# Several changes at once to a tuned attention-plus-MLP kernel: early identity matmuls, 128-wide K/Q transposes, 64-row score tiles, a product in spare PSUM, and new orders of work

## The chip, the cores and the metric

One core of one Trainium2 chip. The metric is device time in microseconds (us), as the median of several executions. PE is the matmul engine, PEld its weight loads, DVE the vector engine, ACT the activation engine, POOL the general engine that also issues the casting DMAs, SP the engine that issues the other DMAs. Ratios are the mean time of one kernel's fast runs over the mean of the other's fast runs of the same rounds, so they are not quite the ratios of the medians quoted.

## The reference

Block-sparse attention (4 batches, 8 heads, 768 positions of 64 values, blocks of 32), followed by a two-layer MLP with exact gelu on its output.

```
mask = |block_i - block_j| <= 1, or either block is the first or the last,
       or block_j is one of 3 sampled blocks of block_i
attn = softmax(where(mask, q @ k.T / 8, -1e9)) @ v         # per batch and head
x    = attn, heads side by side: 3072 x 512
out  = gelu(x @ w_in) @ w_out                              # w_in 512 x 2048, w_out 2048 x 512
```

## The kernel before

Work is cut into eight halves of a batch (384 rows). While PE does the MLP of half n, it also does the attention of half n+1, and POOL gathers K and V blocks for the halves after that. Each half has an order string, whose tokens are played one after the other and fix each engine's order: `H` is a step of the first MLP product (`hp`), `O` of the second (`op`), `S` scores, `W` weighted values, `D` and `E` scores and values of the two end blocks of queries, `t`/`u` transposes of the next batch's K/Q, `K`/`C` gathers of K and V on POOL, `L` the K/Q loads of a batch (on POOL), `F`/`f` scores of batch 0, `B`/`R` the cast of the next batch's V and its rotated copies.

```python
SPARSE = """
H H Z H H B H O1 H H O1 H O2 S0 O1 t1 K01 O3 W0 S1 O1 t0 X0 O2 W1 u0 S2 ... """

def load_qk(b, which, n):                       # 4 heads of a batch, cast f32 -> bf16 by the DMA
    t = st_pool.tile([P, NPAIR, NT * D], BF16, tag="st", name="st")
    pool.dma_start(out=t, in_=src[b, 4 * n:4 * n + 4].rearrange("h (p j) d -> p h (j d)", j=NT))
    return t                                    # rows of 6 * 64 floats: 1,536 bytes

# transpose_qk: two heads of 64 columns go to the upper and the lower half of PSUM
for j in range(NT):
    for h in range(2):
        pe.transpose(ps[64 * h:64 * h + 64, j, :], pair[:, h, j * D:j * D + D], ident)

# dense_scores: qgl holds the end queries of two heads block-diagonally (POOL copies them there)
for t in range(NT):
    pe.matmul(sd[:, t // 3, t % 3 * P:t % 3 * P + P], lhsT=st["k", hp][:, t * P:t * P + P],
              rhs=qgl[hp], start=True, stop=True)

# hidden_steps: products 0/1 and 2/3 take the two score tiles of PSUM, 4/5 waits for a gelu to free one
def step(m):
    mms(m, range(KIN - 1, KIN) if m < 4 else range(KIN))
    gelu(m)
```

The softmax here doesn't subtract the row's maximum and nothing guards it: scores larger than these inputs give would overflow.

Of the kernel before, what the change touches and what calls it, by code (L numbers as in the profile page):

```python
# [10 lines left out]
F32 = mybir.dt.float32  # L11
BF16 = mybir.dt.bfloat16
# [3 lines left out]
AF = mybir.ActivationFunctionType  # L16
ALU = mybir.AluOpType
AX = mybir.AxisListType

P = 128  # L20
B, H, S, D = 4, 8, 768, 64
BLOCK = 32
NB = S // BLOCK
NT = S // P
NR = 3
# [3 lines left out]
NPAIR = H // 2  # L29
# [9 lines left out]


VCH = (4, 4, 3)


class InOrder:
# [12 lines left out]


OPENING = """
A0 F00 k1 F01 F02 q1 F03 F04 F05 k3 P0 F10 F11 F12 k2 q2 F13 J0 F14 F15 F20 V00 V01 V02 F21 J1 F22 q3 F23 F24 F25 X0 F30 V10 V11 V12 P1 F31 F32 J2 F33 X1 V20 V21 V22 J3 F34 M1 F35 X2 V30 V31 L1 V32 H X3"""  # L60
FIRST = """
H H m0 I0 m1 m2 I1 H H m3 m4 H I2 I3 H H I4 H O2 I5 O1 f00 O2 f01 m5 f02 O2 I6 I7 F03 F04 V00 O1 F05 f10 V01 O1 f11 V02 f12 f13 O2 f14 f15 O1 V10 O1 X0 F20 F21 u0 V11 V12 B F22 F23 V20 O1 t0 f24 f25 O1 X1 V21 O1 f30 F31 u1 V22 F32 O2 t1 f33 F34 O1 V30 f35 K00 X2 O1 I8 O1 V31 V32 Q0 O1 R Q1 H K01 X3 O2"""
SECOND = """
H t2 H u3 t3 C00 H C01 C02 H G H H H M2 H K02 O2 K03 S0 u2 K11 K10 C10 C11 O4 D0 O2 L2 W0 S1 O3 D1 X0 C12 O1 E0 W1 S2 O2 E1 O1 X1 K12 D2 O1 W2 S3 O2 X2 E2 D3 O1 W3 E3 O2 K13 Y X3 O3 H"""
SPARSE = """
H H Z H H B H O1 H H O1 H O2 S0 O1 t1 K01 O3 W0 S1 O1 t0 X0 O2 W1 u0 S2 X1 O1 K00 R O2 C00 O1 C01 C02 u1 W2 S3 O2 X2 O3 W3 H O2 X3 O2"""
DENSE = """
M3 H H t2 u2 H H H t3 u3 H H H O2 K03 K02 O1 L3 K10 S0 O1 C10 O2 D0 O1 G O1 W0 S1 O1 K12 O2 C11 D1 O1 X0 W1 C12 S2 O2 E0 K13 O1 D2 O1 E1 W2 S3 O1 K11 O1 X1 E2 D3 O1 W3 E3 O2 Y X2 O3 X3 H"""
SPARSE2 = """
H H Z H H B H O1 H H O1 H O2 S0 O1 t1 K01 O3 W0 S1 O1 t0 X0 O2 W1 u0 S2 X1 O1 K00 R O2 C00 O1 C01 C02 u1 W2 S3 O2 X2 O3 W3 H O2 X3 O2"""  # L70
DENSE2 = """
H H t2 u2 H H H t3 u3 H H H O2 K03 K02 O1 K10 S0 O1 C10 O2 D0 O1 G O1 W0 S1 O1 K12 O2 C11 D1 O1 X0 W1 C12 S2 O2 E0 K13 O1 D2 O1 E1 W2 S3 O1 K11 O1 X1 E2 D3 O1 W3 E3 O2 Y X2 O3 X3 H"""
LAST_SPARSE = """
H H H Z H O1 H H H H O2 S0 O5 S1 W0 O5 W1 S2 O1 X0 X1 O3 W2 S3 O4 X2 O1 W3 H X3 O2"""
LAST = """
H H H O2 H H O2 H H H O28"""
ORDERS = (OPENING, FIRST, SECOND, SPARSE, DENSE, SPARSE2, DENSE2, LAST_SPARSE, LAST)


# [1 line left out]
def kernel(  # L81
# [34 lines left out]
    def cast(eng, dst, src):  # L116
        (eng.copy if eng is act else eng.tensor_copy)(dst, src)


    def load_qk(b, which, n):  # L120

        t = st_pool.tile([P, NPAIR, NT * D], BF16, tag="st", name="st")
        src = {"q": q, "k": k}[which]
        pool.dma_start(
            out=t, in_=src[b, 4 * n:4 * n + 4].rearrange("h (p j) d -> p h (j d)", j=NT))
        return t

    def load_v(b, eng):
# [41 lines left out]
    def small(name, shape, dtype=F32, home=msk):  # L170
        return home.tile([P] + shape, dtype, name=name)
# [11 lines left out]
    iota(blocks, [[1, NB]], 0, 0)  # L183


    kg_all = small("kg_all", [2, NPAIR, NQH, P], BF16, const)
    pt_all = small("pt_all", [2, 2, 2, 512], BF16, const)
    onehot = pt_all[:, 0].rearrange("p a h c -> p (a h c)")[:, 0:NB * BLOCK]
# [18 lines left out]
    dve.memset(seen[:, NB - 1:NB], 1.0)  # L207

    kgl = [[small(f"kgl{i}{hp}", [P], BF16, const) for hp in range(NPAIR)] for i in range(2)]
    qgl = [small(f"qgl{hp}", [P], BF16, const) for hp in range(NPAIR)]  # L210
    vgl = [small(f"vgl{i}", [NPAIR, 2 * VW], BF16, const) for i in range(2)]
    n_all = (NAT1 + NT) * H * GW
    v_flat = small("v_flat", [2 * -(-n_all // DW) * DW], BF16, const)
# [6 lines left out]
    dve.tensor_copy(raw_b, raw[:, :, :, 0].rearrange("p n s -> p (n s)"))  # L220
    ps_raw = mm_pool.tile([P, NB * NR], F32, tag="mm", name="ps_raw")
    pe.matmul(ps_raw, lhsT=ones, rhs=raw_b, start=True, stop=True)
    dve.tensor_copy(sbf.rearrange("p n s -> p (n s)"), ps_raw)
    dve.tensor_scalar(hit, sbf, key_b[:, 0:1], None, op0=ALU.is_equal)
    for s in range(NR):
        dve.tensor_add(seen, seen, hit[:, :, s])
    dve.tensor_scalar(barred.rearrange("p (n c) -> p n c", c=BLOCK),
                      seen.unsqueeze(2).to_broadcast([P, NB, BLOCK]),
                      0.5, -30000.0, op0=ALU.is_lt, op1=ALU.mult)

    lane_i = small("lane_i", [4], I32)
    lane = small("lane", [4])
# [25 lines left out]
                       in_=v[0, 4 * i:4 * i + 4].rearrange("h (p j) d -> p h (j d)", j=NT))  # L258
    for c in range(2):
        load_w_in(c)  # L260
    dve.memset(v_own[0][:, :, :, D:2 * GW], 1.0)

    def first_own(hp):
        r = slice(2 * hp, 2 * hp + 2)
        dve.tensor_copy(v_own[0][:, :, r, 0:D],
                        first_v[:, r].rearrange("p h (j d) -> p j h d", d=D))
# [150 lines left out]
    def transpose_qk(b, hp, which, pair, eng, st):  # L417

        dst = qkt_pool.tile([P, S], BF16, tag=f"t{which}", name=f"t{which}")
        home = (og_pool, "og") if b == 0 and which == "q" else (mm_pool, "mm")  # L420
        ps = home[0].tile([P, NT, P], BF16, tag=home[1], name="ps")
        for j in range(NT):
            for h in range(2):
                pe.transpose(ps[64 * h:64 * h + 64, j, :], pair[:, h, j * D:j * D + D], ident)
        if b == 0 and which == "k":
            to, frm, n = dst.rearrange("p (j n) -> p j n", j=NT), ps, NT
        else:
            to, frm, n = dst.rearrange("p (n j) -> p n j", j=NT), ps.rearrange("p j n -> p n j"), P
        for e, lo, hi in eng if isinstance(eng, tuple) else ((eng, 0, 1),):
            c = slice(int(lo * n), int(hi * n))  # L430
            cast(e, to[:, c], frm[:, c])
        st[which, hp] = dst

    def globals_qk(b, hp, which, eng, st):
        gl = kgl[b % 2][hp] if which == "k" else qgl[hp]
        for i in range(2):
            rs = slice(64 * i, 64 * i + 64)
            cast(eng, gl[rs, rs].rearrange("p (n c) -> p n c", n=2),
                 st[which, hp][rs, :].rearrange("p (n c) -> p n c", c=BLOCK)[:, 0::NB - 1, :])

    def gather_k(b, hb, hp, st):
        kg = st["kg", hb, hp] = kg_all[:, hb, hp]
# [37 lines left out]
    def dense_scores(hp, st):  # L480

        pd = p_pool.tile([P, NT, P], BF16, tag="pd", name="pd")
        sd = sc_pool.tile([P, 2, 512], F32, tag="sc", name="sd")
        for t in range(NT):
            pe.matmul(sd[:, t // 3, t % 3 * P:t % 3 * P + P], lhsT=st["k", hp][:, t * P:t * P + P],
                      rhs=qgl[hp], start=True, stop=True)
        act.activation(pd.rearrange("p (a t) c -> p a (t c)", a=2), sd[:, :, 0:3 * P],
                       AF.Exp, scale=scale)
        st["pd", hp] = pd

    def normalise(dst, og, n):
# [115 lines left out]
    def hidden_steps(b, hb, st):  # L607
        xT = st["xT", hb]

        held = {}  # L610

        def mms(m, kis):
            if 0 in kis:
                held[m] = sc_pool.tile([P, 2, 512], F32, tag="sc", name="hp")
            for i in range(2):
                for ki in kis:
                    pe.matmul(held[m][:, i, 0:HALF], lhsT=w_in_sb[:, ki, (m + i) * P:(m + i + 1) * P],
                              rhs=xT[:, ki, :], start=(ki == 0), stop=(ki == KIN - 1))

        def gelu(m):  # L620
            if m == 0:
                st["g", hb] = g_pool.tile([P, KOUT, HALF], BF16, tag="g", name="g")
            act.activation(st["g", hb][:, m:m + 2, :], held.pop(m)[:, :, 0:HALF], AF.Gelu)

        def begin():
            for m in (0, 2):
                mms(m, range(KIN - 1))

        def step(m):
            mms(m, range(KIN - 1, KIN) if m < 4 else range(KIN))  # L630
            gelu(m)

        return [begin] + [lambda m=m: step(m) for m in range(0, KOUT, 2)]

# [32 lines left out]
    def first_pair(hp, which="kq"):  # L667
        for w in which:
            pair = st["st", w, hp // 2][:, 2 * (hp % 2):2 * (hp % 2) + 2, :]
            if hp == 0:  # L670
                cast(act if w == "k" else dve, pair, first_st[w])
        for w in which:
            pair = st["st", w, hp // 2][:, 2 * (hp % 2):2 * (hp % 2) + 2, :]
            transpose_qk(0, hp, w, pair, (((dve, 0, 1 / 3), (act, 1 / 3, 1)) if w == "k" else ((dve, 0, .5), (act, .5, 1)))
                         if hp == 0 else dve, st)
# [4 lines left out]
                sts[b]["st", w, n] = load_qk(b, w, n)  # L680

    def transpose_next(b, hp, w):
        transpose_qk(b, hp, w, sts[b]["st", w, hp // 2][:, 2 * (hp % 2):2 * (hp % 2) + 2, :],
                     dve, sts[b])
        globals_qk(b, hp, w, pool, sts[b])

    def own_step(b):
        for i in range(2):
# [11 lines left out]
        sts[b]["st", "v"] = load_v(b, pool if b == 1 else sp)  # L700

    def clear_keys():
        for t in kgl[0] + kgl[1] + qgl:
            dve.memset(t, 0.0)

    def clear_values():
# [102 lines left out]
```

## Time and profile before

288.22 us is the median of 3 runs (288.1 to 288.62). The page's first part gives busy time, share of the span and instruction count of each engine:

```profile
PE 265.4 (93%) x3453; PEld 163.5 (57%) x3495; DVE 142.0 (50%) x375; ACT 162.5 (57%) x215; POOL 95.1 (33%) x134
```

PE is the engine to look at, but busy PE time is not PE at its peak, so the main reading was of steps: the time from the start of a group of matmuls to the start of the next group. The timeline of PE shows two matmul groups around a set of K transposes (start, length, engine, operation, count):

```profile
119.66 0.38 PE L54 MATMUL op<-w_out_sb,g 128*128 128x512 bf16 x1
119.97 0.53 PE L54 MATMUL ps<-ident,st 128*64 128x128 bf16 x12
120.43 0.82 PE L54 MATMUL op<-w_out_sb,g 128*128 128x512 bf16 x3
```

Twelve half-width transposes hold PE from 119.97 to 120.43, 0.46 us, of which the last one alone accounts for 0.15 (a tail of 0.12; the others step 0.028 each). The `op` matmul ahead of them takes 0.31 us to the next start, where others take 0.216. So here a change between full-width and half-width tiles cost about 0.09 us before the group and 0.12 after it.

The waits view, for PE (who waited for whom: total us, times, longest), in its first rows:

```profile
PE ps_raw L54 <- DVE raw_b L54: 3.7, 1, 3.7
PE hp L54 <- ACT g L54: 2.5, 5, 0.6
```

All its PE rows together are 15.0 us. The second row is the third product waiting for a gelu to free a score tile: 0.57 us early in each of four halves (2, 4, 6 and 7), and 0.2 us some 7 us into half 1.

POOL's timeline around the load of batch 2 (the bracket is the idle time before, and what ended it; "issue" is time in which nothing that the profile shows was waited for):

```profile
109.57 1.65 POOL L54 INDIRECT_COPY v_gat<-v_flat,idx_v 128x1024 f32 x1 [1.99 <-issue]
111.17 0.79 POOL L54 DMA_DIRECT2D st<-in_k_dram  x1
111.96 0.76 POOL L54 DMA_DIRECT2D st<-in_q_dram  x1
112.70 0.77 POOL L54 DMA_DIRECT2D st<-in_k_dram  x1
113.43 0.78 POOL L54 DMA_DIRECT2D st<-in_q_dram  x1
115.55 1.45 POOL L54 INDIRECT_COPY v_gat<-v_flat,idx_v 128x768 f32 x1 [1.34 <-issue]
```

Four loads take 3.1 us. A gather occupies POOL for about 3.6 us with its "issue" time (1.65 + 1.99), although only 1.65 of that counts as busy.

### The profile page before, as it was taken

Reading aid. Unit: us, or ns where it says so; the run is one execution under the profiler, and the core shown is the slowest. Engines: PE = TensorE matmul, PEld = TensorE weight load, DVE = VectorE, ACT = ScalarE, POOL = GpSimd, SP = SyncE. Lnnn points to the kernel's source line nnn. Section 1 sums busy time; section 2 is a strip of 40 time slices with the busy share of each in tenths; the row PEclk is TensorE's granted clock in tenths of the full one; section 3 lists DMA queues with packets and bytes.
Section 4 is the critical chain, followed back from the end, with each engine's and each line's share of the span. In section 5 each row is a group of like instructions: output and inputs, shape, how many; then the busy total and the mean of one; then the engine's idle time right before and its main releaser. Section 6 shows DMA issues by size and latency. Waiting matters only on the chain.

```text
span 286.8 us, 7929 instructions
## 1 busy us (share of the span) xinstructions
PE 265.4 (93%) x3453; PEld 163.5 (57%) x3495; DVE 142.0 (50%) x375; ACT 162.5 (57%) x215; POOL 95.1 (33%) x134
## 2 busy tenths in 40 slices
PE   1999799999799999999999999999998999999995
PEld 1466454465456765566566755566555755565544
DVE  7255498898804670486325652465326560153002
ACT  3698558774367555744467635654466635845420
POOL 8400830013444336334273534231453333100000
PEclk9999999999999999999999999999999999999999
DMA  7999999209891003969580970088000100000101
GB/s 167 238 250 209 209 234 201 58 2 237 219 181 39 11 33 70 186 155 257 128 137 37 135 163 2 3 201 217 37 2 37 41 37 2 25 35 19 39 37 73
DMA packets 30036, 31.27 MB, mean 109 GB/s; under 512 B 13649, under 2 KB 24146, under 8 KB 30002
## 3 DMA queue, kind: packets, MB, share of 16 engines
q0 software_dynamic: 11936, 13.24, 26.5%
q1 hardware_dynamic: 18064, 17.53, 23.4%
q8 instruction: 27, 0.44, 0.6%
q14 instruction: 7, 0.06, 0.1%
q10 hardware_dynamic: 2, 0.00, 0.0%
HBM read 27.26 MB, written 6.29 MB: 117 GB/s over the span
## 4 chain that ended last, share of the span: by engine, by line
PE 60%; DVE 16%; issue 11%; POOL 7%; ACT 5%; POOLq 0%; DVEq 0%; ACTq 0%
PE hp L54 21%; PE op L54 18%; PE s L54 7%; PE og L54 6%; PE ps L54 4%; POOL kg_all L54 3%; POOL v_gat L54 2%; DVE v_flat L54 2%; PE psx L54 2%; DVE v_gat L54 1%; ACT L54 1%; ACT g L54 1%; POOL st L54 1%; PE od L54 1%; ACT kg_all L54 1%
## 5 line engine op out<-in xcount | busy, mean ns | idle before, releaser
L54 PE MATMUL op<-w_out_sb,g 128*128 128x512 bf16 (+1 forms) x358 | 89.8, 370 | 2.2 <-issue 0.2
L54 PE MATMUL hp<-xT,w_in_sb 128*128 128x384 bf16 x512 | 88.5, 326 | 2.9 <-ACT g L54 2.5
L54 ACT ACTIVATE g<-hp 128x768 bf16<-128x768 f32 x64 | 51.0, 810 | 61.1 <-PE hp L54 61.0
L54 PEld LDWEIGHTS <-w_in_sb 128*128 128x128 bf16 x512 | 49.1, 98 | 38.3 <-issue 5.2
L54 ACT ACTIVATE pt_all<-s 128x1024 bf16<-128x1024 f32 (+2 forms) x72 | 44.2, 687 | 30.4 <-PE s L54 30.3
L54 PEld LDWEIGHTS <-g 128*128 128x128 bf16 x400 | 35.6, 98 | 27.4 <-issue 1.6
L54 POOL INDIRECT_COPY kg_all<-tk,idx_k 128x704 f32 x24 | 30.3, 1262 | 58.8 <-issue 53.9
L54 DVE TENSOR_TENSOR pt_all<-pt_all,mask_x 128x768 bf16<-128x768 bf16 x24 | 14.7, 614 | 56.5 <-ACT pt_all L54 56.5
L54 POOL INDIRECT_COPY v_gat<-v_flat,idx_v 128x1024 f32 (+1 forms) x18 | 28.5, 1581 | 39.7 <-issue 16.4
L54 DVE COPY os<-op 128x512 f32<-128x512 f32 (+1 forms) x25 | 16.7, 667 | 21.5 <-PE op L54 20.9
L54 PEld LDWEIGHTS <-pt_all 128*32 128x32 bf16 (+2 forms) x818 | 22.0, 99 | 9.0 <-issue 2.9
L54 PE MATMUL s<-tq,tk 64*128 64x128 bf16 (+1 forms) x240 | 24.6, 272 | 1.2 <-DVE tq L54 0.7
L54 ACT ACT_TABLE_LOAD x16 | 20.5, 1283 | 8.0 <-PE hp L54 6.5
L54 PEld LDWEIGHTS <-tk 64*128 64x128 bf16 (+1 forms) x312 | 14.1, 96 | 14.0 <-issue 9.0
L54 PEld LDWEIGHTS <-st 128*64 128x64 bf16 x384 | 12.9, 118 | 14.1 <-issue 8.3
L54 ACT ACTIVATE kg_all<-s 128x768 bf16<-128x768 f32 x24 | 17.9, 814 | 4.9 <-PE s L54 4.9
L54 PE MATMUL ps<-ident,st 128*64 128x128 bf16 x384 | 17.4, 236 | 2.8 <-DVE st L54 1.4
L54 ACT ACTIVATE v_gat<-s 128x768 bf16<-128x768 f32 x24 | 18.1, 813 | 3.1 <-PE s L54 2.9
L54 DVE COPY tk<-ps 128x768 bf16<-128x768 bf16 (+1 forms) x16 | 13.4, 835 | 11.3 <-PE ps L54 11.2
L54 DVE TENSOR_TENSOR x<-og,rc 128x384 bf16<-128x384 f32 x32 | 17.8, 557 | 1.1
L54 DVE CAST v_flat<-st_v 128x1536 bf16<-128x1536 f32 (+1 forms) x10 | 8.9, 917 | 17.4 <-POOL v_gat L54 17.4
L54 DVE COPY tq<-ps 128x768 bf16<-128x768 bf16 (+1 forms) x16 | 14.8, 926 | 3.2 <-PE ps L54 3.2
(119 smaller groups left out, 244.7 us busy)
## 6 DMA issues: line engine op xcount, KB each, us to landing
out_dram<-os SPq DMA_DIRECT2D x23, 256.0 KB, 2.1
v_flat<-v_flat SPq DMA_DIRECT2D x6, 594.0 KB, 7.0
st_v<-in_v_dram SPq DMA_DIRECT2D x12, 256.0 KB, 4.9
st<-in_k_dram POOLq DMA_DIRECT2D x7, 384.0 KB, 7.2
st<-in_q_dram POOLq DMA_DIRECT2D x7, 384.0 KB, 8.4
v_flat<-v_flat SPq DMA_DIRECT2D x6, 396.0 KB, 5.2
w_in_sb<-in_moe_w_in_dram POOLq DMA_DIRECT2D x2, 1024.0 KB, 18.1
w_out_sb<-in_moe_w_out_dram POOLq DMA_DIRECT2D x2, 1024.0 KB, 26.7
```

The source lines that it names most:

```text
L54: return self._tc.keep_in_program_order(f(*args, **kwargs))
```

## The change

Its intent: keep PE active with identity matmuls before the first keys arrive, so that its clock is raised early; load K/Q of batches 2 and 3 with two heads side by side, so that six full transposes replace twelve half-width ones; compute the end blocks' scores as pairs of 64-row tiles, which needs no `qgl` copies; compute the third MLP product in PSUM banks that the output and the transposes use, so that it need not wait for gelu. It also splits the first Q cast between ACT and DVE, shortens the mask sum and moves `barred` behind them, and rewrites all nine order strings (with 11 instead of 14 tiles masked by DVE). The core of the diff:

```diff
+WIDE = 2
 SPARSE = """
-H H Z H H B H O1 H H O1 H O2 S0 O1 t1 K01 O3 W0 S1 O1 t0 X0 O2 W1 u0 S2 X1 O1 K00 R O2 C00 ...
+H H H H H u0 t1 H O1 Z H H O1 B O1 S0 O3 R K01 O2 S1 O2 W0 t0 W1 O2 S2 K00 O2 X0 C00 ...
 ... (the other eight orders likewise)
@@ load_qk
-        pool.dma_start(
-            out=t, in_=src[b, 4 * n:4 * n + 4].rearrange("h (p j) d -> p h (j d)", j=NT))
+        if b < WIDE:
+            pool.dma_start(
+                out=t, in_=src[b, 4 * n:4 * n + 4].rearrange("h (p j) d -> p h (j d)", j=NT))
+            return t
+        t = t.rearrange("p n c -> p (n c)").rearrange("p (a j h d) -> p a j h d", a=2, j=NT, h=2)
+        for a in range(2):
+            pool.dma_start(out=t[:, a], in_=src[b, 4 * n + 2 * a:4 * n + 2 * a + 2].rearrange(
+                "h (p j) d -> p j h d", j=NT))
         return t
@@ after the identity is made; 9 more after the first matmul
+    warm = og_pool.tile([P, P], F32, tag="og", name="warm")
+    def warm_up(n):
+        for _ in range(n):
+            pe.matmul(warm, lhsT=ident, rhs=ident, start=True, stop=True)
+    warm_up(19)
@@ transpose_qk
         for j in range(NT):
+            if b >= WIDE:
+                pe.transpose(ps[:, j, :], pair[:, j].rearrange("p h d -> p (h d)"), ident)
+                continue
             for h in range(2):
@@ dense_scores
-            pe.matmul(sd[:, t // 3, t % 3 * P:t % 3 * P + P], lhsT=st["k", hp][:, t * P:t * P + P],
-                      rhs=qgl[hp], start=True, stop=True)
+            for h in range(2):
+                r = slice(64 * h, 64 * h + 64)
+                pe.matmul(sd[:, h, 64 * t:64 * t + 64],
+                          lhsT=st["k", hp][r, t * P:t * P + P], rhs=ends[r], start=True, stop=True)
@@ hidden_steps
+        def lone(m):
+            t = mm_pool.tile([P, D_MODEL], F32, tag="mm", name="hp")
+            for ki in range(KIN):
+                pe.matmul(t[:, 0:HALF], lhsT=w_in_sb[:, ki, m * P:m * P + P], rhs=xT[:, ki, :],
+                          start=(ki == 0), stop=(ki == KIN - 1))
+            gelu(m, 1, t[:, 0:HALF])
         def step(m):
+            if m == 4:
+                lone(4)
+                lone(5)
+                return
 ... (opening casts, mask sum, removal of qgl: cut)
```

More of the change, by code (lines that the diff above doesn't have):

```diff
@@ L59 @@
 OPENING = """
-A0 F00 k1 F01 F02 q1 F03 F04 F05 k3 P0 F10 F11 F12 k2 q2 F13 J0 F14 F15 F20 V00 V01 V02 F21 J1 F22 q3 F23 F24 F25 X0 F30 V10 V11 V12 P1 F31 F32 J2 F33 X1 V20 V21 V22 J3 F34 M1 F35 X2 V30 V31 L1 V32 H X3"""
+A0 F00 F01 P0 F02 F03 q1 F04 k1 F05 k3 F10 F11 k2 F12 q2 F13 J0 F14 F15 F20 V00 V01 V02 F21 F22 F23 q3 P1 F24 F25 J1 X0 F30 V10 V11 V12 F31 F32 F33 J2 X1 V20 V21 V22 F34 J3 F35 M1 X2 V30 L1 V31 V32 H X3"""
 FIRST = """
-H H m0 I0 m1 m2 I1 H H m3 m4 H I2 I3 H H I4 H O2 I5 O1 f00 O2 f01 m5 f02 O2 I6 I7 F03 F04 V00 O1 F05 f10 V01 O1 f11 V02 f12 f13 O2 f14 f15 O1 V10 O1 X0 F20 F21 u0 V11 V12 B F22 F23 V20 O1 t0 f24 f25 O1 X1 V21 O1 f30 F31 u1 V22 F32 O2 t1 f33 F34 O1 V30 f35 K00 X2 O1 I8 O1 V31 V32 Q0 O1 R Q1 H K01 X3 O2"""
+m0 m1 H H m2 I0 H H I1 m3 m4 H H H I2 H I3 I4 m5 I5 f00 O5 f01 I6 O1 F02 I7 O1 F03 F04 O1 V00 F05 f10 O1 V01 f11 V02 f12 F13 O2 f14 f15 O2 X0 u0 F20 F21 V10 V11 B V12 F22 f23 t0 O1 V20 f24 F25 O2 f30 X1 V21 F31 u1 F32 V22 t1 f33 F34 V30 O3 R O1 I8 V31 F35 X2 O2 V32 H K00 Q1 O1 X3 O1 Q0 K01"""
@@ L63 @@
 SECOND = """
-H t2 H u3 t3 C00 H C01 C02 H G H H H M2 H K02 O2 K03 S0 u2 K11 K10 C10 C11 O4 D0 O2 L2 W0 S1 O3 D1 X0 C12 O1 E0 W1 S2 O2 E1 O1 X1 K12 D2 O1 W2 S3 O2 X2 E2 D3 O1 W3 E3 O2 K13 Y X3 O3 H"""
+u3 H t2 C00 G H H C01 H H H M2 C02 t3 H H O2 S0 O4 S1 K02 W0 K03 u2 L2 C10 D0 K10 O1 C11 K11 D1 O1 X0 E0 O2 C12 S2 K12 O1 W1 O1 D2 W2 E1 O1 X1 O1 K13 O1 X2 O1 E2 S3 O4 D3 W3 O1 E3 O1 Y X3 O2 H"""
 SPARSE = """
-H H Z H H B H O1 H H O1 H O2 S0 O1 t1 K01 O3 W0 S1 O1 t0 X0 O2 W1 u0 S2 X1 O1 K00 R O2 C00 O1 C01 C02 u1 W2 S3 O2 X2 O3 W3 H O2 X3 O2"""
+H H H H H u0 t1 H O1 Z H H O1 B O1 S0 O3 R K01 O2 S1 O2 W0 t0 W1 O2 S2 K00 O2 X0 C00 O1 u1 X1 O1 C01 C02 W2 S3 O3 X2 O2 W3 O3 X3 H"""
@@ L67 @@
 DENSE = """
-M3 H H t2 u2 H H H t3 u3 H H H O2 K03 K02 O1 L3 K10 S0 O1 C10 O2 D0 O1 G O1 W0 S1 O1 K12 O2 C11 D1 O1 X0 W1 C12 S2 O2 E0 K13 O1 D2 O1 E1 W2 S3 O1 K11 O1 X1 E2 D3 O1 W3 E3 O2 Y X2 O3 X3 H"""
+C10 H H H H u2 t2 K02 H H H t3 H K03 O1 G O1 S0 u3 O2 M3 O1 D0 L3 O1 C11 W0 K12 S1 K10 O1 E0 K11 O1 C12 O3 D1 D2 W1 X0 O1 S2 E1 O4 W2 S3 E2 O2 D3 O1 W3 K13 E3 O2 X1 Y X2 O3 X3 H"""
 SPARSE2 = """
-H H Z H H B H O1 H H O1 H O2 S0 O1 t1 K01 O3 W0 S1 O1 t0 X0 O2 W1 u0 S2 X1 O1 K00 R O2 C00 O1 C01 C02 u1 W2 S3 O2 X2 O3 W3 H O2 X3 O2"""
+H H H H H u0 t1 H O1 Z H H O1 B O1 S0 O3 R K01 O2 S1 O2 W0 t0 W1 O2 S2 K00 O2 X0 C00 O1 u1 X1 O1 C01 C02 W2 S3 O3 X2 O2 W3 O3 X3 H"""
@@ L71 @@
 DENSE2 = """
-H H t2 u2 H H H t3 u3 H H H O2 K03 K02 O1 K10 S0 O1 C10 O2 D0 O1 G O1 W0 S1 O1 K12 O2 C11 D1 O1 X0 W1 C12 S2 O2 E0 K13 O1 D2 O1 E1 W2 S3 O1 K11 O1 X1 E2 D3 O1 W3 E3 O2 Y X2 O3 X3 H"""
+C10 H H H H u2 t2 K02 H H H t3 H K03 O1 G O1 S0 u3 O3 D0 O1 C11 W0 K12 S1 K10 O1 E0 K11 O1 C12 O3 D1 D2 W1 X0 O1 S2 E1 O4 W2 S3 E2 O2 D3 O1 W3 K13 E3 O2 X1 Y X2 O3 X3 H"""
 LAST_SPARSE = """
-H H H Z H O1 H H H H O2 S0 O5 S1 W0 O5 W1 S2 O1 X0 X1 O3 W2 S3 O4 X2 O1 W3 H X3 O2"""
+H H H H H O1 H O1 H H O3 S0 O5 S1 O3 W0 S2 O2 X0 O1 W1 S3 O1 X1 W2 O2 W3 Z X2 O2 X3 O3 H"""
@@ L75 @@
 LAST = """
-H H H O2 H H O2 H H H O28"""
+H H H H H O3 H O1 H H O28"""
 ORDERS = (OPENING, FIRST, SECOND, SPARSE, DENSE, SPARSE2, DENSE2, LAST_SPARSE, LAST)
@@ L209 @@
     kgl = [[small(f"kgl{i}{hp}", [P], BF16, const) for hp in range(NPAIR)] for i in range(2)]
-    qgl = [small(f"qgl{hp}", [P], BF16, const) for hp in range(NPAIR)]
     vgl = [small(f"vgl{i}", [NPAIR, 2 * VW], BF16, const) for i in range(2)]
@@ L222, with bar @@
     pe.matmul(ps_raw, lhsT=ones, rhs=raw_b, start=True, stop=True)
+    warm_up(9)
     dve.tensor_copy(sbf.rearrange("p n s -> p (n s)"), ps_raw)
     dve.tensor_scalar(hit, sbf, key_b[:, 0:1], None, op0=ALU.is_equal)
-    for s in range(NR):
-        dve.tensor_add(seen, seen, hit[:, :, s])
-    dve.tensor_scalar(barred.rearrange("p (n c) -> p n c", c=BLOCK),
-                      seen.unsqueeze(2).to_broadcast([P, NB, BLOCK]),
-                      0.5, -30000.0, op0=ALU.is_lt, op1=ALU.mult)
+    met = small("met", [NB])
+    dve.tensor_reduce(met, hit, op=ALU.max, axis=AX.X)
+    dve.tensor_add(seen, seen, met)
+    def bar():
+        dve.tensor_scalar(barred.rearrange("p (n c) -> p n c", c=BLOCK),
+                          seen.unsqueeze(2).to_broadcast([P, NB, BLOCK]),
+                          0.5, -30000.0, op0=ALU.is_lt, op1=ALU.mult)
     lane_i = small("lane_i", [4], I32)
@@ L260 @@
         load_w_in(c)
-    dve.memset(v_own[0][:, :, :, D:2 * GW], 1.0)
     def first_own(hp):
+        if hp == 0:
+            dve.memset(v_own[0][:, :, :, D:2 * GW], 1.0)
         r = slice(2 * hp, 2 * hp + 2)
@@ L432, in transpose_qk, with globals_k @@
         st[which, hp] = dst
-    def globals_qk(b, hp, which, eng, st):
-        gl = kgl[b % 2][hp] if which == "k" else qgl[hp]
+    def globals_k(b, hp, eng, st):
+        gl = kgl[b % 2][hp]
         for i in range(2):
@@ L438, in globals_qk @@
             cast(eng, gl[rs, rs].rearrange("p (n c) -> p n c", n=2),
-                 st[which, hp][rs, :].rearrange("p (n c) -> p n c", c=BLOCK)[:, 0::NB - 1, :])
+                 st["k", hp][rs, :].rearrange("p (n c) -> p n c", c=BLOCK)[:, 0::NB - 1, :])
     def gather_k(b, hb, hp, st):
@@ L483, in dense_scores @@
         sd = sc_pool.tile([P, 2, 512], F32, tag="sc", name="sd")
+        ends = st["q", hp].rearrange("p (n c) -> p n c", c=BLOCK)[:, 0::NB - 1, :]
         for t in range(NT):
-            pe.matmul(sd[:, t // 3, t % 3 * P:t % 3 * P + P], lhsT=st["k", hp][:, t * P:t * P + P],
-                      rhs=qgl[hp], start=True, stop=True)
-        act.activation(pd.rearrange("p (a t) c -> p a (t c)", a=2), sd[:, :, 0:3 * P],
-                       AF.Exp, scale=scale)
+            for h in range(2):
+                r = slice(64 * h, 64 * h + 64)
+                pe.matmul(sd[:, h, 64 * t:64 * t + 64],
+                          lhsT=st["k", hp][r, t * P:t * P + P], rhs=ends[r],
+                          start=True, stop=True)
+        act.activation(pd.rearrange("p t (h c) -> p h t c", h=2),
+                       sd[:, :, 0:3 * P].rearrange("p h (t c) -> p h t c", t=NT), AF.Exp, scale=scale)
         st["pd", hp] = pd
@@ L618, in mms, with gelu @@
                               rhs=xT[:, ki, :], start=(ki == 0), stop=(ki == KIN - 1))
-        def gelu(m):
+        def gelu(m, n, src):
             if m == 0:
                 st["g", hb] = g_pool.tile([P, KOUT, HALF], BF16, tag="g", name="g")
-            act.activation(st["g", hb][:, m:m + 2, :], held.pop(m)[:, :, 0:HALF], AF.Gelu)
+            act.activation(st["g", hb][:, m:m + n, :], src, AF.Gelu)
+        def lone(m):
[4 more added lines that the diff above has]
+            gelu(m, 1, t[:, 0:HALF])
         def begin():
@@ L629, in step @@
         def step(m):
+            if m == 4:
+                lone(4)
+                lone(5)
+                return
             mms(m, range(KIN - 1, KIN) if m < 4 else range(KIN))
-            gelu(m)
+            gelu(m, 2, held.pop(m)[:, :, 0:HALF])
         return [begin] + [lambda m=m: step(m) for m in range(0, KOUT, 2)]
@@ L670, in first_pair @@
             if hp == 0:
-                cast(act if w == "k" else dve, pair, first_st[w])
+                act.copy(pair[:, 0:2 if w == "k" else 1], first_st[w][:, 0:2 if w == "k" else 1])
+        if hp == 0:
+            dve.tensor_copy(st["st", "q", 0][:, 1], first_st["q"][:, 1])
+            bar()
         for w in which:
@@ L682, in transpose_next @@
     def transpose_next(b, hp, w):
-        transpose_qk(b, hp, w, sts[b]["st", w, hp // 2][:, 2 * (hp % 2):2 * (hp % 2) + 2, :],
-                     dve, sts[b])
-        globals_qk(b, hp, w, pool, sts[b])
+        transpose_qk(b, hp, w, sts[b]["st", w, hp // 2][:, hp % 2] if b >= WIDE
+                     else sts[b]["st", w, hp // 2][:, 2 * (hp % 2):2 * (hp % 2) + 2, :], dve, sts[b])
+        if w == "k":
+            globals_k(b, hp, pool, sts[b])
     def own_step(b):
@@ L702, in clear_keys @@
     def clear_keys():
-        for t in kgl[0] + kgl[1] + qgl:
+        for t in kgl[0] + kgl[1]:
             dve.memset(t, 0.0)
```

## The prediction

> **What bounds the kernel.** PE is busy 265.4 of 286.8 us (page, part 1); of the chain that ended last it has 60%, DVE 16%, POOL and "issue" 18%. I cut the span at the first `hp` matmul of each half and took start-to-start steps from the timeline. From 106 to 261 us PE loses only 3 to 4 us to waits. Slack lies early: the opening (to 30.4 us) holds 17 us of PE work; 30 to 70 us loses about 7 us, with DVE busy 37.9 of 45.4 us (windows view, 30.6 to 76).
>
> **Opening.** The first score matmuls start at 8.36, the first exp at 9.22 us. DVE makes `barred` (0.88) and casts Q (0.73) before it copies `tk` at 6.73, although K's transposes ended at 5.5. Until 14.1 us four score matmuls take 0.64 us, afterwards 0.325: this agrees with the Trainium skill ("TensorE: Matmul & The Clock Gate", Part 1) that matmuls start at half rate and speed up after sustained activity, though the PEclk row reads full. After that ACT limits: 24 exps of 0.74 us, with 2.6 us of gaps. Warm-up, split Q cast, shorter mask sum and F01 to F03 first should start the exps near 8 us and close most gaps: -2.5 us. The clock may still rise late, as PE waits for copies again after the warm-up.
>
> **30 to 76 us.** Three masked tiles fewer on DVE (about 0.5 us each), no `qgl` memsets (0.33), new order; PE gets 3 x 0.16 us more. I expect -3 us.
>
> **Wide transposes.** A group of 12 half-width transposes takes 0.46 us, 0.123 of it a tail, and the matmul before it 0.093 more than its like; 12 more in one group cost 0.34. This agrees with "TensorEngine Tiling (Array Packing)", Tiling Modes, Key Properties: changing the tiling mode drains the array. Full `psx` transposes step 0.056 us, so six take 0.336 (estimate). For batches 2 and 3: 8 single groups x 0.22 + 4 double x 0.22 = -2.6 us, nearly all on PE's path.
>
> **End scores.** Six full matmuls take 0.335 us; six pairs at about 0.03 plus two mode changes of 0.09 make 0.36 (estimate): nothing gained on PE. POOL's `qgl` copies (5.6 us in all) go.
>
> **Third product.** PE waits 0.5 us for gelu at five half starts (`hp`<-ACT g, 2.5 us in the waits view). A bank outside the score pool takes most away: -2 us.
>
> **Cost: POOL and DMA.** K/Q loads of batches 2, 3 become 128-byte rows, six times as many; 8 issues per batch, about 1.0 us each (estimate from 0.88 for 1,024-row V loads) instead of 4 x 0.77: +5 us of POOL per batch, less 2 us of `qgl`. POOL runs gathers back to back (3.4 to 3.6 us with issue) from 146 to 187 us and already makes PE wait 0.9 us at 185.6. I expect 1 to 3 us of new waits for `kg_all` or `v_gat`, mainly in the sparse half after batch 3's load.
>
> **Sum.** -2.5 -3 -2.6 -2 +2: 288.2 falls to 280.8, range 276 to 286. Faster by over 2%: 0.65; within 2%: 0.33; slower: 0.02.
>
> **Right if:** first exp near 8 us; `ps` groups of batches 2 and 3 step 0.056 without the tail; `hp`<-ACT waits under 1 us; `sd` groups still about 0.35 us. **Wrong if:** slow K/Q packets make `ps` wait for loads, POOL delays pass 3 us, or DVE still paces 30 to 70 us.

## The result and the profile after

291.03 us is the median of 4 runs (290.49 to 291.14), against 288.16 for the kernel before. The ratio is 1.0097 (95% interval 1.0074 to 1.0121): 1% slower, where 2.6% faster was forecast and 286 was the upper end of the range.

The span, cut at the first `hp` matmul of each half, in us. The last column adds the PE rows of the waits view. The lower rows are experiments that come further down.

| kernel | opening | half 0 | 1 | 2 (sparse) | 3 (dense) | 4 (sparse) | 5 (dense) | 6 | 7 and end | PE waits |
|---|---|---|---|---|---|---|---|---|---|---|
| before | 30.4 | 39.7 | 35.6 | 28.5 | 34.5 | 29.5 | 35.1 | 27.3 | 26.2 | 15.0 |
| after | 28.5 | 39.2 | 35.3 | **34.7** | 32.2 | **35.7** | 31.8 | 27.5 | 24.4 | 17.3 |
| e12: after, short-row loads undone | 28.5 | 39.3 | 35.2 | 29.6 | 32.8 | 29.6 | 32.5 | 27.5 | 24.4 | 6.4 |
| e5: e12 and three more gathers per load block | 28.2 | 39.2 | 35.3 | 35.7 | 32.4 | 35.7 | 32.5 | 27.5 | 24.4 | 13.5 |
| e7: e12, third product waits again | 28.1 | 39.9 | 37.4 | 30.7 | 33.2 | 30.5 | 33.2 | 28.2 | 25.2 | 13.6 |
| e9: e12 with the old orders | 27.9 | 40.0 | 36.2 | 29.5 | 37.1 | 27.8 | 35.4 | 26.6 | 26.0 | 13.3 |

Each row is one profiled execution. How far two executions differ can be seen from e1, which is the same kernel as e12: its opening takes 27.7 us and its half 2 30.6, so differences below 1 us in one cell prove little.

The change won about 2 us each in the opening, in half 3 and at the end, and 3 in half 5, and lost 6.2 us in each of the two sparse halves.

The page's first part, after:

```profile
PE 266.3 (92%) x3465; PEld 164.8 (57%) x3505; DVE 137.8 (48%) x367; ACT 162.6 (56%) x224; POOL 137.8 (48%) x118
```

POOL's busy time has grown by 43 us, with fewer instructions. Its timeline at the load of batch 2 shows why (to be read against the six lines of before):

```profile
91.30 1.19 POOL L55 INDIRECT_COPY kg_all<-tk,idx_k 128x704 f32 x1 [2.08 <-issue]
92.44 3.25 POOL L55 DMA_DIRECT2D st<-in_k_dram  x2
94.53 4.53 POOL L55 DMA_DIRECT2D st<-in_q_dram  x2
96.53 5.90 POOL L55 DMA_DIRECT2D st<-in_k_dram  x2
98.53 7.27 POOL L55 DMA_DIRECT2D st<-in_q_dram  x2
102.61 6.87 POOL L55 INDIRECT_COPY v_gat<-v_flat,idx_v 128x1024 f32 x1
106.34 6.31 POOL L55 INDIRECT_COPY kg_all<-tk,idx_k 128x704 f32 x1
109.54 6.70 POOL L55 INDIRECT_COPY v_gat<-v_flat,idx_v 128x1024 f32 x1
113.27 6.14 POOL L55 INDIRECT_COPY kg_all<-tk,idx_k 128x704 f32 x1
115.79 6.33 POOL L55 INDIRECT_COPY v_gat<-v_flat,idx_v 128x768 f32 x1
```

Read the ends, not the starts. The eight loads start every 1.0 us, but the last one ends at 98.53 + 7.27 = 105.80: POOL was held for 13.4 us, 1.67 us per load, and starts ran ahead of the work. The five gathers behind them start on time and end at 109.48, 112.65, 116.24, 119.41 and 122.12, one after the other, 2.7 to 3.7 us apart, as fast as ever. Their lengths of 6 us are mostly queueing, and so are POOL's additional "busy" us.

What PE felt of it, in the timeline of half 2:

```profile
120.88 0.33 PE L55 MATMUL og<-vgl,pt_all 128*128 128x130 bf16 x3
122.15 1.91 DVE L55 CAST v_flat<-st_v 128x1536 bf16<-128x1536 f32 x2 [9.44 <-POOL v_gat L55]
123.97 0.58 DVE L55 TENSOR_TENSOR pt_all<-pt_all,mask_x 128x768 bf16<-128x768 bf16 x1
...
124.62 0.51 PE L55 MATMUL og<-v_flat,pt_all 128*128 128x65 bf16 x6 [3.40 <-DVE pt_all L55]
```

PE has begun the first weighted sum and needs masked scores; DVE's mask product stands behind the cast of the next batch's V, which overwrites rows that the late V gather (end 122.12) still reads. The same happens at about 189 us in half 4. Over the whole run the waits view has

```profile
PE og L55 <- DVE pt_all L55: 7.0, 3, 3.4
PE s L55 <- POOL kg_all L55: 2.1, 2, 1.4
```

The second row is PE waiting for K gathers, once in each sparse half. Neither row is in e12. The windows view adds a second loss (length, busy us of PE, PEld, DVE, ACT and POOL, then the granted PE clock, DMA share and GB/s):

```profile
120.90:124.40 3.50, 0.31 (x4) 0.14 (x2) 2.25 (x3) 1.10 (x3) 3.50 (x3) 1.00 0.00 0
124.40:127.90 3.50, 2.95 (x66) 2.63 (x68) 3.27 (x8) 0.00 (x0) 3.50 (x3) 0.51 0.79 179
```

After the idle stretch PE gets half its clock for 3.41 us (the length of the clock record), once in each of the two halves. In that time a group of 22 small `og` matmuls takes 0.45 us to the next start (125.06 to 125.51) instead of 0.29. This agrees with the Trainium skill, "TensorE: Matmul & The Clock Gate", Part 1, which gives a window of 3,413 ns after which an idle PE drops to half rate: here PE stood idle for 3.40 and 3.36 us (from matmul ends that the trace models). At most 2 x 1.7 us are lost that way (an estimate from the two records), so here the waiting PE lost more than the wait.

What the change was meant to do to the transposes, it did. PE's timeline, two wide groups in a row:

```profile
109.48 0.83 PE L55 MATMUL ps<-ident,st 128*128 128x128 bf16 x12
110.16 0.81 PE L55 MATMUL hp<-xT,w_in_sb 128*128 128x384 bf16 x4
```

Twelve step 0.68 us, 0.34 per group, and nothing is left of the tail.

### The profile page after: what moved, and what is told of

Its sections match the earlier page's. It is cut to its first block, busy times and chain, and to the rows that moved or that the text cites. A ratio compares the mean times of both kernels' runs of the same rounds, so it can differ in the third digit from the quotient of the medians.

```text
span 289.3 us, 7931 instructions
## 1 busy us (share of the span) xinstructions
PE 266.3 (92%) x3465; PEld 164.8 (57%) x3505; DVE 137.8 (48%) x367; ACT 162.6 (56%) x224; POOL 137.8 (48%) x118
## 4 chain that ended last, share of the span: by engine, by line
PE 47%; POOL 25%; DVE 11%; issue 8%; DMA 7%; ACT 0%; POOLq 0%; SPq 0%; DVEq 0%
PE hp L55 15%; PE op L55 15%; POOL st L55 9%; POOL v_gat L55 8%; POOL kg_all L55 7%; PE og L55 6%; PE s L55 5%; DMA st_v<-in_v_dram 3%; DMA v_flat<-v_flat 2%; PE ps L55 2%; DVE v_flat L55 2%; PE psx L55 1%; DMA st<-in_k_dram 1%; DVE mask_x L55 1%; DVE v_gat L55 1%
## 5 line engine op out<-in xcount | busy, mean ns | idle before, releaser
L55 ACT ACTIVATE g<-hp 128x768 bf16<-128x768 f32 (+1 forms) x72 | 50.8, 742 | 56.4 <-PE hp L55 56.1
L55 POOL INDIRECT_COPY kg_all<-tk,idx_k 128x704 f32 x24 | 63.5, 3052 | 36.1 <-issue 31.6
L55 ACT ACTIVATE pt_all<-s 128x1024 bf16<-128x1024 f32 (+2 forms) x72 | 44.2, 686 | 39.7 <-PE s L55 36.0
L55 POOL INDIRECT_COPY v_gat<-v_flat,idx_v 128x1024 f32 (+1 forms) x18 | 53.5, 2995 | 26.8 <-issue 18.9
L55 DVE TENSOR_TENSOR pt_all<-pt_all,mask_x 128x768 bf16<-128x768 bf16 x24 | 13.8, 575 | 42.4 <-ACT pt_all L55 42.4
L55 PEld LDWEIGHTS <-pt_all 128*32 128x32 bf16 (+2 forms) x824 | 23.6, 103 | 15.1 <-DVE pt_all L55 7.5
L55 POOL COPY kgl<-tk 64x64 bf16<-64x64 bf16 x24 | 18.5, 770 | 23.5 <-DVE tk L55 21.5
L55 POOL DMA_DIRECT2D st<-in_q_dram x12 | 25.9, 3329 | 4.8 <-DMA w_out_sb<-in_moe_w_out_dram 4.4
L55 POOL DMA_DIRECT2D st<-in_k_dram x12 | 21.5, 2414 | 1.4 <-DMA w_out_sb<-in_moe_w_out_dram 0.9
L55 PEld LDWEIGHTS <-tk 64*128 64x128 bf16 x384 | 11.9, 94 | 17.9 <-issue 14.5
L55 DVE COPY tk<-ps 128x768 bf16<-128x768 bf16 (+1 forms) x16 | 13.4, 836 | 12.7 <-PE ps L55 12.7
```

Source lines behind the costliest of these rows:

```text
L55: return self._tc.keep_in_program_order(f(*args, **kwargs))
```

## The experiments

Twelve kernels ran; all gave correct results. "Time" is a median; ratios are to the kernel before, run in the same rounds.

### e1_narrow: the short-row loads and wide transposes undone

```diff
-WIDE = 2
+WIDE = 4
```

> The changed kernel, with the K/Q loads and the transposes of batches 2 and 3 as they were before (1,536-byte source rows, two heads transposed apart); everything else of the change stays. Theory 1 (the eight loads of short rows hold POOL for 13.3 us instead of 3.1 per batch, the gathers queue behind them and PE waits in the two sparse halves): the two sparse halves, 34.7 and 35.7 us after the change, fall to about 29.5 each, the dense halves grow by about 0.5, and the time is 281 to 283 us. Theory 2 (the new order of work asks for the gathers too early, whatever the loads are): the halves keep most of their waits and the time stays at 288 us or more.

Measured: 281.73 us, ratio 0.9784 (0.9745 to 0.9823). The sparse halves fell to 30.6 and 29.7 us and the dense ones grew by 0.2 and 0.7. The short-row loads and the wide transposes that they were for had cost 9 us together, and all the rest together gains 6.5 us. Theory 1 stands, theory 2 falls. POOL's timeline for the load of batch 2 is again what it was before the change:

```profile
90.85 0.80 POOL L55 DMA_DIRECT2D st<-in_k_dram  x1
91.64 0.75 POOL L55 DMA_DIRECT2D st<-in_q_dram  x1
92.38 0.76 POOL L55 DMA_DIRECT2D st<-in_k_dram  x1
93.11 0.77 POOL L55 DMA_DIRECT2D st<-in_q_dram  x1
```

### e2_gathers and e5_gathers2: POOL's time alone

On e1, three more gathers (repeats, same result) behind each late load stand for the time that short rows had taken, without any short row.

```diff
                 sts[b]["st", w, n] = load_qk(b, w, n)
+        if b >= 2:
+            for _ in range(3):
+                gather_k(b - 1, 0, 3, sts[b - 1])        # e2;  e5: gather_k(b - 1, 0, 0, ...)
```

> As e1_narrow, but three more runs of a K gather that POOL has just made (same result, no DMA) follow each of the two late load blocks: about 3 x 3.2 = 9.6 us of POOL, as much as the short rows added. Theory 1a (it is POOL's time alone that counts): back to 288 to 292 us, with the waits of the changed kernel in the sparse halves. Theory 1b (it is the DMA traffic of short rows, late arrivals or crowded queues): within 1.5 us of e1_narrow.

Measured: 299.33 us, ratio 1.0414 (1.0376 to 1.0453). This test was badly made: the repeats rewrote the K blocks of head pair 3, whose scores were still to come, so PE waited for the repeats themselves (13.1 us in two waits of `s` for `kg_all`, in halves 1 and 3, where the changed kernel has none of that size). It says nothing of the theories.

> The same test as e2_gathers with its fault taken away: there the repeated gather wrote a tile that a score product still to come read, so that PE waited for the repeats themselves. Here the three repeats write the tile of the first head pair, whose reader is done, so that only POOL's later gathers are delayed, by about 10 us per late load block, and the K/Q loads keep long rows. POOL's time alone: 288 to 293 us, with waits in the sparse halves (34 us or so instead of 30) and none of 5 us or more in the halves before. Short DMA rows needed for the loss: 281 to 283.5 us.

Measured: 292.71 us, ratio 1.0129 (1.0097 to 1.0162). Halves 2 and 4 take 35.7 us each, as in the changed kernel, and the waits view has the same row as there:

```profile
PE og L55 <- DVE pt_all L55: 6.9, 2, 3.5
```

The clock drops behind those waits too (half rate for 6.83 us in half 2 and 3.41 in half 4). So the loss needs no short row in the DMA queues; holding POOL for some 10 us per batch is enough.

### e3_late_own: the blocking cast moved

```diff
-... Z H H O1 B O1 S0 O3 R K01 O2 S1 O2 W0 t0 W1 ...
+... Z H H O1 O1 S0 O3 K01 O2 S1 O2 W0 B R t0 W1 ...        (both sparse halves)
```

> The changed kernel with its wide loads, but in the two sparse halves DVE casts the next batch's V rows, and their rotations start, only after the first weighted sum. In the changed kernel that cast waits 9.4 us for a V gather on POOL and stands ahead of the mask product that PE's weighted sum needs. If that blocking adds to POOL's lateness: 286 to 288.5 us, PE's longest wait in those halves falling from 3.5 to about 1.5 us. If PE waits for the gather itself in any case: within 1 us of 291.

Measured: 292.38 us (one of four runs at 288.48), ratio 1.0102 (1.002 to 1.0185), no gain on the change's 1.0097. PE now waits for the gathers directly, on K gathers for 9.2 us and on a V gather (`og` for `v_gat`) for 1.4:

```profile
PE s L55 <- POOL kg_all L55: 9.2, 6, 4.1
```

The sparse halves take 34.0 and 35.6 us, hardly less than the changed kernel's 34.7 and 35.7 (and half 5 grew from 31.8 to 34.2, for a reason that was not looked into). DVE's cast was only the messenger; the late gathers are the cause.

### e4_side_copy and e8_side_early: wide transposes without short rows

With long rows the two heads of a pair lie 384 elements apart in SBUF; here DVE copies them side by side first. In e8 that copy comes four pieces of work ahead of the transposes.

```diff
+            side = x_pool.tile([P, NT, 2, D], BF16, tag="side", name="side")
+            dve.tensor_copy(side, pair.rearrange("p h (j d) -> p j h d", d=D))
```

> Wide transposes without short rows: the loads of e1_narrow, and a DVE copy inside SBUF puts the two heads side by side before six full transposes. If PE time is what the halves of batches 1 and 2 are made of, it gains on e1_narrow what the change meant to gain: 1 to 2.5 us less, 279 to 281 us. If POOL's gathers pace those halves, or the copies (16 of about 0.4 us, estimate) delay DVE, no gain: within 0.5 us of e1_narrow or slower.

Measured: 300.74 us, ratio 1.0451 (1.0395 to 1.0507). The saving on PE is there, but PE stood still for it, as the waits view says:

```profile
PE ps L55 <- DVE side L55: 17.3, 10, 2.4
```

> e4_side_copy with each DVE copy four pieces of work earlier in the order. In e4_side_copy PE waited 17.3 us in all for copies that came right ahead of their transposes. If that lack of lead was the loss: PE waits for copies under 3 us in all, and the time 279 to 282 us, where e1_narrow had 281.7. If DVE has no room for 16 copies of about 0.45 us in these halves: still over 285 us.

Measured: 280.78 us, ratio 0.9711 (0.9674 to 0.9747). The same row is down to 1.7 us:

```profile
PE ps L55 <- DVE side L55: 1.7, 2, 1.2
```

Lead was what e4 lacked. This is the fastest kernel measured, 2.9% faster than before. Its interval just overlaps that of e12 (0.9741 to 0.9806), which ran in another set of rounds, so its gain over e12 is likely but small, less than the 2.6 us that the prediction expects the transposes to save on PE: PE's waits sum to 10.9 us here and to 6.4 in e12. (In the profiled execution halves 2 to 5 even took 126.0 us against 124.5, but that execution, 282.43 us, is one of e8's two slowest.)

### e6_no_warm: without the identity matmuls

```diff
-    warm_up(19)
-    warm_up(9)
```

> e1_narrow without the 28 identity matmuls. If the early full clock (raised at 4.7 us instead of 14.6) is what shortened the opening: the opening grows from 27.7 to 29 us or more, the time by 1 to 2.5 us on e1_narrow (281.7). If key loads and ACT pace the opening whatever PE's rate is: within 0.7 us of e1_narrow.

Measured: 281.38 us, ratio 0.9742 (0.9715 to 0.9768); e12, with them, has 281.84 and 0.9774. They gain nothing. They do raise the clock early, if not each time: of the eleven profiled kernels that have them, the clock record begins at 4.7 to 6.3 us in eight and at 10.1 to 10.5 in three; without them it begins at 10.7 here, at 13.7 in e11 and at 14.6 in the kernel before. It makes no difference: the opening takes 28.2 to 28.4 us in the three and 27.7 to 29.1 in the eight. The first exps, from ACT's timeline, of the changed kernel and of e6:

```profile
7.10 4.33 ACT L55 ACTIVATE kg_all<-s 128x768 bf16<-128x768 f32 x6
```

```profile
7.85 2.92 ACT L55 ACTIVATE kg_all<-s 128x768 bf16<-128x768 f32 x4 [0.40 <-PE s L55]
```

The lead of 0.75 us is gone by the end of the opening: the last of its 24 exps starts at 26.88 and 26.78 us. In between, the changed kernel's PE waited 1.8 us for keys, up to 12.07 us:

```profile
PE ps L55 <- DMA st<-in_k_dram: 1.8, 1, 1.8
```

So PE's clock did not shorten the opening. Nor is the new order needed for it: e9 below, with the old orders, opens in 27.9 us. What it shares with the others is the split Q cast, the shorter mask sum and the later `barred`; no run separates these.

### e7_no_lone and e11_before_lone: the third product, taken out and put in alone

```diff
-            if m == 4:          # e7: out of e1;  e11: lone() put into the kernel before
-                lone(4)
-                lone(5)
-                return
```

> e1_narrow with the third product again in a score bank, so that it waits for the first gelu. As the prediction had it, 0.5 us for each of some seven half starts, and more because the new order starts the halves with five steps of the product in a row: 2 to 6 us more than e1_narrow, and hp waits for ACT g return. If other work hides the wait: less than 1 us more.

Measured: 289.58 us, ratio 1.0019 (0.9975 to 1.0063), 7.7 us more than e12 by the medians, about 7 by the ratios (e12 ran in other rounds). The waits are back, once in each of the eight halves:

```profile
PE hp L55 <- ACT g L55: 5.8, 8, 1.4
```

> The kernel before with one part of the change: the third product in spare PSUM, all orders as they were. The prediction's account of it (2.5 us of waits for gelu, most of them gone): 285.5 to 287 us where before has 288.4. If the part only pays with an order that puts five steps of the product at the start of a half: within 0.7 us of before.

Measured: 289.08 us, ratio 1.0046 (1.0004 to 1.0088): alone, it gains nothing. The waits of `hp` for gelu are gone from its trace, but PE's waits still sum to 15.2 us; in half 3 they grew from 0.2 to 2.5 us, and the half from 34.5 to 37.3. Part of them is new and shows what "spare" meant: the two banks also take the transposes, and the old order puts those right ahead of the product.

```profile
PE hp L54 <- DVE tk L54: 1.4, 2, 0.7
```

### e9_old_orders: the parts without the new order

e1 with the nine order strings of before; nothing else differs.

> e1_narrow with the nine order strings of the kernel before (three more masked tiles with them); warm-up, quicker opening, third product and end scores stay. If the parts themselves carry the gain: 281 to 283.5 us, as e1_narrow. If the new order is needed to use them: 285 to 288 us.

Measured: 288.11 us, ratio 0.9987 (0.9947 to 1.0027). All parts together gain nothing in the old order, though the opening alone is 2.5 us shorter; half 3 is 2.7 us longer than before. With e7 this makes a clear table (medians in us; e7, e9 and e12 have all other parts of the change and the long rows, e11 has no other part):

| | third product in score tiles | third product in spare PSUM |
|---|---|---|
| old orders | 288.2 (before) | 288.1 (e9), 289.1 (e11) |
| new orders | 289.6 (e7) | 281.8 (e12) |

Neither half of the pair is worth anything without the other, for these two sets of orders (the new set masks three tiles fewer on DVE). The new orders start a half with five product steps in a row; that pays only if the third one needs no gelu, and the third one's freedom pays only if the order uses it. PE's waits after the opening say the same: 7.5 us before, 8.7 in e9, 7.7 in e11, 8.8 in e7 and, with both, 1.2 in e12.

### e10_full_ends: the end scores at full height again

```diff
-            for h in range(2):  ... 64-row products of the end queries
+                pe.matmul(sd[:, t // 3, ...], lhsT=st["k", hp][:, t * P:t * P + P], rhs=qgl[hp], ...)
+        globals_qk(b, hp, w, pool, sts[b])       # POOL copies the end queries again
```

> e1_narrow with the end blocks' scores again as six full matmuls and POOL's copies of the end queries back (5.6 us of POOL in all). From the trace of the changed kernel twelve half-height products take 0.282 us plus 0.095 before them, against 0.335: full height saves PE 0.5 us in all. If only PE counts: within 0.7 us of e1_narrow, rather faster. If POOL has no room for its copies: more than 1 us slower.

Measured: 281.34 us, ratio 0.9752 (0.9721 to 0.9784), beside e12's 281.84 and 0.9774. No difference to be seen, in either direction.

### e12_narrow_again: e1 once more

> e1_narrow once more, beside the three others and in five rounds, to compare with them and with e6 to e8: 281 to 282.5 us.

Measured: 281.84 us, ratio 0.9774 (0.9741 to 0.9806), as e1. It is the comparison for e6 to e11; only e9 to e11 ran in its rounds, so e6 to e8 are compared by their ratios.

## Why the prediction was wrong

- **"Cost: POOL and DMA" is the step that failed.** It put the eight short-row loads at "about 1.0 us each", so "+5 us of POOL per batch", and "1 to 3 us of new waits" in all. They start 1.0 us apart, but hold POOL for 1.67 us each: 13.4 us per batch instead of 3.1, so +10.3. The prediction had itself found POOL working back to back; instead of its 1 to 3 us of new waits PE got 9.1 us (7.0 for `pt_all`, held up by a V gather, and 2.1 for `kg_all`). The sparse halves grew by 5.1 and 6.1 us against e12, where the loads are undone (34.7 - 29.6 and 35.7 - 29.6), partly by the clock drop that the waits set off, which the prediction did not think of. The parts nearly add up: 3.40 + 0.71 us of waits and up to 1.7 of half clock (the estimate above) in half 2, 3.36 + 1.41 and up to 1.7 in half 4. Its "wrong if: POOL delays pass 3 us" named the right place.
- **The estimate's fault** was to carry the cost of one kind of load (1,024 rows of 256 bytes uncast, 0.88 us) to another (1,536 rows, cast, four-dimensional). Why the latter takes 1.67 us, by its rows, its access pattern or a wait for the DMA queue, no run separates; it stays open. Two things in the trace speak against some answers: the eight ends lie 1.7 us apart each time, while their data land 1.25 to 3.5 us apart; and loads of `w_out`, 1,024 rows and cast as well, take 0.97 us in the kernel before.
- **Wide transposes, -2.6 us:** right on PE (0.34 us per group, no tail). In time it shows as 0.2 to 0.7 us per dense half (after against e1 and e12), and e8, which pays with DVE copies instead, is about 0.6% faster than e12 by the ratios.
- **Third product, -2 us:** wrong by itself (e11: nothing gained), too small in company (e7: 7.7 us). The waits view showed 2.5 us of waits to remove; it can't show that others take their place in the old order (e11), or that their removal lets another order in (e12).
- **Reordering had no term of its own.** The prediction names the order only inside its terms for the opening and for 30 to 76 us. With the third product it was worth 6.3 us (288.11 - 281.84), and without it nothing (e7). The pair was the largest gain of the change.
- **Without the loads and wide transposes** the prediction's other terms, -2.5 - 3 - 2, give 280.7 us, and e12 measured 281.84. That is luck: halves 0 and 1 gave 0.9 us of the 3, and the pair of product and order made up for it.
- **30 to 76 us, -3 us:** halves 0 and 1 gained 0.5 and 0.4 us. Fewer masked tiles did not make them shorter; what paces them was not tested.
- **Opening, -2.5 us:** measured -1.9, with the first exp at 7.10 instead of "near 8". Its doubt, that the clock may still rise late, did not come true in the changed kernel's trace (4.97 us) but did in three others of eleven; e6 shows that it does not matter, as the warm-up is worth nothing here.
- **End scores:** PE takes 0.282 us per group and 0.095 ahead of it, 0.38 against the 0.36 expected and 0.335 before; no effect on the time (e10), as predicted.

## What to carry to other kernels

Before a load is reshaped to please PE, cost it on the engine that issues it, by when the work behind it ends and not by how often it starts, above all where that engine's queue is what the next stage waits for. A buffer that frees one product and an order that exploits the freedom have to be tried together: each alone measured nothing here, and with both (and the shorter opening) the kernel was 2.3% faster than before. When a change bundles several ideas, undo them one at a time: here one bad part hid a kernel faster than both.

## What the Trainium skill lacked or had wrong

- "DMA: Bandwidth & Descriptors", Anatomy of one DMA, calls the time to generate descriptors "small, variable" and says that many can be emitted before the extra cost shows. Here eight loads of 1,536 short rows each held POOL for 13.4 us, 1.67 us each, against 0.77 us for loads of 512 long rows. Whether descriptors are the reason, no run shows.
- "Perfetto Trace Analysis", GPSIMD Engine Instruction, warns that POOL's spans are unreliable and advises to time its instructions by the spacing of their starts. For these DMA issues that misleads: starts came every 1.0 us, ends every 1.7 and up to 6.3 us behind, and the gathers queued after them were shown with 6.1 to 6.9 us instead of 1.2 to 1.7.
- "TensorE: Matmul & The Clock Gate", Part 1: the half-rate window agrees (3.41 us behind waits of 3.40 and 3.36 us; 6.83 us, two windows, behind one of 3.48 us in e5). The advice of its last part, "Why this matters for your kernels", to keep PE busy for 4 us or more, gained nothing in this opening (e6: 281.38 us without, 281.84 with). 28 small matmuls, from 1.4 to 4.9 us with short gaps, raised the clock by 6.3 us in only eight of eleven profiles; the page itself says that the moment varies.
- "TensorEngine Tiling (Array Packing)", Key Properties, says that a change of tiling mode drains PE and gives no figure: here 0.09 us ahead of a group of transposes and 0.12 behind it.
